# Masked k by small DMAs, scores in any two PSUM banks, and a new order: a four-layer attention and FFN kernel

## The chip, the cores and the metric

The kernel runs on one core of a Trainium2 chip. The metric is the device time of one execution in microseconds (us), as a median of several runs. Five engines have instruction queues of their own: TensorE (PE; its weight loads are shown as PEld), VectorE (DVE), ScalarE (ACT), GpSimd (POOL) and SyncE (SP), which here only issues DMAs.

## The reference

Four layers work on `x` of 2048 rows and 512 columns in bfloat16: attention with a memory, a gated FFN, and both again. Each adds to `x`, and each begins with a layer norm. Cut to what matters:

```python
def _A_ref(x, wq, wk, wv, wo, beta):          # 32 heads of 16, N = 4 segments of L = 512 rows
    q, k, v = ...                              # x @ wq, x @ wk, x @ wv, by head and segment
    phi = lambda t: jnp.where(t > 0, t + 1.0, jnp.exp(t))
    mask = (ar[:, None] < ar[None, :]) * -1e9  # causal inside a segment
    g = sigmoid(beta)
    M, z = 0, 0
    for s in range(N):
        p = softmax(qs @ ks.T * scale + mask)
        a_dot = p @ vs
        a_mem = (phi(qs) @ M) / (phi(qs) @ z + 1e-6)
        outs.append(g * a_mem + (1.0 - g) * a_dot)
        M = M + phi(ks).T @ vs
        z = z + phi(ks).sum(0)
    return concat(outs) @ wo

def _B_ref(x, w_gate, w_up, w_down):           # inner width 1792
    return gelu(x @ w_gate) * (x @ w_up) @ w_down

x = x + _A_ref(layernorm(x), ...)
x = x + _B_ref(layernorm(x), ...)
x = x + _A_ref(layernorm(x), ...)
x = x + _B_ref(layernorm(x), ...)
```

Both attention layers share their weights, and so do both FFNs.

## The kernel before

**Tiles.** `x_sb` holds the whole `x`, and all weights stay in SBUF. The work is cut into eight parts, k = 0 to 7: two layer pairs of four segments of 512 rows each. A part has an attention (class `Att`) and an FFN (class `Ffn`). A 512x512 projection is done in four blocks b of 128 columns; a block holds eight heads of 16.

**Scores.** A head has 16 rows of its block, and four heads are multiplied at once in four row groups of TensorE. The even heads of a block stand at rows 32j to 32j+15, so they use 16 rows of `kf` directly. The odd heads use 32 rows of `kB`, a copy of `kf` in which the rows of the even heads are zero. Before, `k_done` makes that copy on GpSimd: it multiplies the 128x512 block by the column `maskB` (L539), after the block's eviction from PSUM. `score_ready` demands it for the odd heads alone. For k = 0, `q`, `kf` and `kB` lie in `wd_sb`, which is loaded later; other parts rotate over three sets.

**From scores to output.** Rounds of scores go into pairs of PSUM banks; two rounds fill two pairs. Before, a pair is banks 2p and 2p+1 (`ps_pairs`). ScalarE takes the exponential of a pair in one instruction over 1024 columns (L1199), GpSimd zeroes the part above the diagonal (`affine_select`, L1205), and a "flush" multiplies five rounds by v (L809). DVE transposes and divides the result (L824 to L839) and adds the memory's part (L842). `wo` adds to `x_sb` (L879). Rows are then normed: statistics on DVE (L405, L413), a power on GpSimd (`rs`, L418 and L423), and `xn` on DVE (L435). `xn` is transposed into `xnT` by a DMA on SP (`turn_later`), or on TensorE for three of the parts (L467).

**phi.** `e` = exp on ScalarE (L596), cut at 1 by GpSimd or DVE (L614; `phi_pool` tells below which part it is DVE), and summed with the positive part on DVE (L600). phi of k is transposed by DMA (`phik`), and so is the memory's output (`amT`).

**FFN.** Gate products are evicted to `gel_sb` by DVE or ScalarE (L366, L367; `evict` leaves it to whichever is planned to be first) and then turned into gelus over several tiles at once (`gelu_tiles`, L991). The last `direct` gates of a part take the gelu straight from PSUM (L917). Products with up are multiplied on DVE (L939).

**What sets the order.** All engines run in an order that `order` writes out before the program is built. It keeps a clock for each engine (`Engine`, `Clocks`), posts each step with a planned duration and a slack, and lets each engine take what comes next by planned time. TensorE goes on as long as an item is ready and a bank free. If nothing is, it emits a dummy matmul on `warm` (a "fill"). Products run in the array's tiling at that moment: whole (L379) or as four column groups of 32 (L376); scores use row groups (L793), flushes column groups. The numbers of `POLICY` are slacks and due times of the planner. On the chip the order is fixed, and semaphores do the waiting; SP's DMAs too are issued strictly in the planned order, and nearly all of them on one queue.

Of the kernel before, what the change touches and what calls it, by code (L numbers as in the profile page):

```python
# [54 lines left out]
    flush_wait=-1.813, piece_slack=1.086, kb_slack=2.08, mem_slack=-2.073, margin=1.389, qk_due=0.513,  # L55
    e_q=-0.257, e_k=1.032, exp_slack=0.902, e_slack=10.959, phi_slack=4.283, gelu_slack=1.187, act_evict=3.627,
    first_evict=4.817, gate_step=0.01, up_due=0.388, up_step=0.027, down_due=2.499, down_step=0.058,
    upd_due=-0.151, v0_due=-1.527, x1_at=10.541, x2_at=16.065, x3_at=40.015, cut_slack=6.049, direct=1,
    gelu_tiles=3, kb_dve=0, phi_pool=1, rounds=2, early=1, starve=0.518, cap=4, fuse=1)


class Engine:
# [4 lines left out]
    def __init__(self, overlap=0.0):  # L67
        self.free, self.overlap, self.jobs, self.table = 0.0, overlap, [], "exp"
        self.only = None
# [17 lines left out]
    def serve(self, now):  # L87

        self.jobs = [j for j in self.jobs if not j[4]]
        jobs = [j for j in self.jobs if not self.only or j[3] in (None, self.only)]  # L90
        if not jobs:
            return False
        start = max(self.free, min(j[0] for j in jobs) + self.LATENCY)
        if start > now:
            return False
        job = min((j for j in jobs if j[0] + self.LATENCY <= start + 0.03), key=lambda j: j[0] + j[1])
        ready, _, steps, table, taken = job
        taken.append(1)
        self.jobs.remove(job)
        t = ready  # L100
        if table and table != self.table:
            self.free += 1.28
            self.table = table
        for cost, emit, told in steps:
            t = max(self.free, t + self.LATENCY) + cost
            self.free = t - self.overlap
            if emit:
                emit()
            if told:
                told(t)  # L110
        return True


class Clocks:
# [6 lines left out]
    def __init__(self):  # L121
        self.pe = 0.0
        self.mode = "whole"
        self.act, self.dve, self.pool, self.sp = Engine(0.09), Engine(0.07), Engine(), Engine()
        self.engines = (self.dve, self.act, self.pool, self.sp)
        self.later, self.seq, self.waiting = [], 0, []
        self.dma, self.fills, self.stalls = 0.0, [], []
        self.ev = {}
# [103 lines left out]
def order(pol, nc, cst, seg, wrk, psp, A_x, A_wq, A_wk, A_wv, A_wo, A_beta, B_x, B_w_gate, B_w_up, B_w_down, out):  # L232
# [34 lines left out]
    pieces = [(14.0, 512, lambda: load_x(2)), (27.0, 512, lambda: load_x(3))]  # L267
# [17 lines left out]
    nc.vector.memset(warm[:], 1.0)  # L285

    ps_all = psp.tile([P, BANKS, L], F32, tag="ps", bufs=1, name="ps")
    ps_pairs = ps_all[:].rearrange("p (a b) c -> p a (b c)", b=2)
# [20 lines left out]
    maskB = cst.tile([P, 1], F32, name="maskB")  # L309
    nc.vector.reduce_sum(out=maskB[:], in_=bd[:, 16:P:32], axis=mybir.AxisListType.X)  # L310
# [81 lines left out]
    class Norm:  # L392
# [46 lines left out]
        def row(self, j, i, ready):  # L439
            xn = Box(lambda: self.normed(j, i))  # L440

            def landed(t):
                xn_slots.back(i, t)
                self.left -= 1
                if not self.left:
                    ev[self.key] = t

            def told(t):
                if self.key in BY_PE:
                    items.append(self.turn_item(j, xn, t, landed))  # L450
                else:
                    turn_later(t, self.slack, lambda: self.xnT[:, :, j * P:(j + 1) * P], lambda: xn()[:], landed,
                           pol.margin)

            ck.dve.post(ready, self.slack, (0.46, xn, told))
# [34 lines left out]
    class Att:  # L490
# [12 lines left out]
        def add_items(self):  # L503
# [5 lines left out]
            def first():  # L509
                if k:  # L510
                    self.q, self.kf, self.kB = (seg.tile([P, KT, L], BF16, tag=f"{n}{k % SETS}", bufs=1, name=n)
                                                for n in ("q", "kf", "kB"))
                else:
                    self.q, self.kf, self.kB = (wd_sb[:, KT * i:KT * (i + 1), :] for i in range(3))
                return True
# [19 lines left out]
            def k_done(b, ps, at=None):  # L535
                def told(t):
                    ev["k", k, b] = t
                    eng, job, cost = (nc.vector, ck.dve, 0.345) if k < pol.kb_dve else (nc.gpsimd, ck.pool, 1.566)
                    job.post(t, pol.kb_slack if k else NORMAL, (cost, lambda: eng.tensor_scalar(  # L539
                        out=self.kB[:, b, :], in0=self.kf[:, b, :], scalar1=maskB[:, 0:1], scalar2=None,  # L540
                        op0=ALU.mult), lambda t2: ev.update({("kB", k, b): t2})))
                    if s < NSEG - 1:
                        before = ("mem", k - 1) if s else ("mem", k - 2) if k else ("xnTa", k + 1)
                        e_jobs.append((k + pol.e_k + 0.03 * b, t, lambda: before in ev,
                                       lambda r, sl: self.phi(b, "k", r, sl)))

                if at is not None:
                    told(at)
                else:
                    evict(ps, lambda: self.kf[:, b, :], lambda: ps()[:], told)  # L550
# [4 lines left out]
            def v(j):  # L555
# [4 lines left out]
                def done():  # L560
# [6 lines left out]
                            lambda: ck.has(("xnTa", k)) and (k <= SETS or ("flush", k - SETS, 3, 1) in ev),  # L567
# [17 lines left out]
        def phi(self, b, which, ready, slack):  # L585
            def take(i):
# [29 lines left out]
                def summed(t):  # L616
                    ck.dve.post(t, pol.phi_slack, (0.75 if which == "q" else 0.83, add, told))

                def made(t):
                    if self.k < pol.phi_pool:  # L620
                        ck.dve.post(t, pol.phi_slack, (0.32, cut(nc.vector), None),
                                    (0.75 if which == "q" else 0.83, add, told))
                    else:
                        ck.pool.post(t, pol.cut_slack, (1.566, cut(nc.gpsimd), summed))
# [154 lines left out]
        def score_round(self, t, places):  # L779
# [5 lines left out]
            for ki, q0, n, c0 in PIECES[i]:  # L785
                for j in range(4):
# [6 lines left out]
                    nc.tensor.matmul(ps_all[:, 2 * pair + unit // 2, o:o + n], lhsT=lhsT[rows, b, P * ki:P * ki + P],  # L793
# [3 lines left out]
        def flush_item(self, b, par, places, masked):  # L797
# [16 lines left out]
            def done():  # L814
# [35 lines left out]
                def put():  # L850
                    steps = [(0.706, back, None if self.s else there)]
                    if self.s:
                        steps.append((0.447, add, there))
# [3 lines left out]
                if par:  # L857
                    steps += [(0.355, inverse, None), (0.7, scale, kept)]
# [185 lines left out]
    first_scale(2, 4)  # L1044
    n0.first_xn = [n0.normed(0, 0), n0.normed(1, 1)]
# [24 lines left out]
    ck.pe, ck.act.free, ck.dve.free, ck.pool.free, ck.sp.free = 8.8, 9.45, 8.9, 6.2, 7.2  # L1070
# [4 lines left out]
    later_constants()  # L1075
    for at, kb, piece in pieces:
# [12 lines left out]
    norm_of_input(1, pol.x1_at, 0.5)  # L1089
    norm_of_input(2, pol.x2_at, 1.0)  # L1090
    norm_of_input(3, pol.x3_at, 1.0)
# [4 lines left out]
    score_pairs = set()  # L1096
# [14 lines left out]
    def free(bank, t):  # L1111
        return banks[bank] <= t

    def free_pairs():
        return [p for p in range(BANKS // 2) if free(2 * p, ck.pe - 0.05) and free(2 * p + 1, ck.pe - 0.05)]
# [4 lines left out]
    def rounds_now():  # L1120

        if not streams:
            return 0
        ready = 0
        for k, t in streams[:pol.rounds]:
            if not att[k].score_ready(t):
                break
            ready += 1
        n = min(len(free_pairs()), len(slot_free), ready)
        if n >= 3 and len(streams) != 4:  # L1130
            return 3
        if n >= 2 and len(streams) != 3 and (streams[0][0] < pol.early or len(streams) in (2, 4) or backlog() < pol.starve):
# [3 lines left out]
    def pick():  # L1136

        got = [i for i in range(BANKS) if free(i, ck.pe)]
        mine = len({i // 2 for i in range(BANKS) if banks[i] > ck.pe and i // 2 not in score_pairs})
        half = [i for i in got if not free(i ^ 1, ck.pe)]  # L1140
        if half:
            return min(half, key=lambda i: (-banks[i ^ 1], banks[i]))
        if got and (mine < pol.cap or not streams):
            return max(got, key=lambda i: i)
        return None
# [8 lines left out]
    def score(n):  # L1154
        pairs = free_pairs()[:n]
# [26 lines left out]
        groups = [[p] for p in range(n)] if n == 2 or not pol.fuse else [[2], [0, 1]] if pol.fuse == 1 else [[0, 1], [2]]  # L1182
        for group in groups:
            jobs, parts = [], []
            for p in group:
                pair, slot = pairs[p], slots[p][1]
                score_pairs.add(pair)
                slot_users[slot] = len(users[p])
                banks[2 * pair] = banks[2 * pair + 1] = 1e9
# [8 lines left out]
            def exp(p0=p0, p1=p1, s0=s0, s1=s1):  # L1198
                nc.scalar.activation(  # L1199
                    out=pt_all[:, s0:s1 + 1:max(s1 - s0, 1), :, :].rearrange("p s u c -> p s (u c)"),  # L1200
                    in_=ps_pairs[:, p0:p1 + 1:max(p1 - p0, 1), :], func=ACT.Exp, scale=SCALE)
# [6 lines left out]
            def told(a, parts=parts, jobs=jobs):  # L1208
                for pair, _ in parts:
                    score_pairs.discard(pair)  # L1210
                    banks[2 * pair] = banks[2 * pair + 1] = a
# [19 lines left out]
    while streams or items or opened or ck.busy():  # L1231
# [16 lines left out]
        if bank is not None:  # L1248
# [6 lines left out]

            if streams:
# [65 lines left out]
```

## Time and profile before

| | |
|---|---|
| Median of 3 runs | 563.16 us (561.08 to 563.27) |
| The profiled execution | 561.81 us, span 560.1 us |
| TensorE busy | 542.6 us (97%), 9193 matmuls |
| DVE busy | 449.8 us (80%) |
| ScalarE busy | 450.9 us (81%) |
| GpSimd busy | 323.8 us (58%) |
| Exponentials of scores (ACT L1199) | 320, mean 1026 ns |
| Masks on the diagonal (POOL L1205) | 320, mean 589 ns |
| Cuts of e on GpSimd (POOL L614) | 44, mean 1520 ns |
| DMA share | 20.1% of 16 engines on the main queue |
| Granted TensorE clock | 1.0 |

The profile is one execution. "Busy" counts an engine's instructions; a wait is idle time. The chain that ended last is followed back from the last instruction, so a share in it says how much of the span hung on that engine. Some matmul records are missing from the trace: 9193 of 9234 are there.

### The profile page before, as it was taken

What the parts mean: (1) busy time and instruction counts of PE and PEld (TensorE: products, weight loads), DVE (VectorE), ACT (ScalarE), POOL (GpSimd) and SP (SyncE); (2) the same over time, 40 slices, a digit from 0 to 9 for tenths busy, and PEclk for the clock granted to TensorE, in tenths of its full rate; (3) what the DMA queues carried; (4) which work ended last, traced back from release to release, by engine and by line L of the source; (5) the groups of instructions that cost most, each with busy time, mean ns of one, the idle gap of its engine ahead of it and who ended that gap; (6) DMA issues with size and microseconds to landing.
All of it is one profiled execution on the core that took longest, in us unless ns stands there. A gap on an engine that the chain in (4) does not pass through costs nothing.

```text
span 560.1 us, 21158 instructions
## 1 busy us (share of the span) xinstructions
PE 542.6 (97%) x9193; PEld 271.0 (48%) x9234; DVE 449.8 (80%) x821; ACT 450.9 (81%) x533; POOL 323.8 (58%) x438
## 2 busy tenths in 40 slices
PE   7999999999999999999999999999999999999997
PEld 3444454444445444444444444445445445555544
DVE  4999899979998699789698887988976877886332
ACT  5899999999798978999999699998899986730230
POOL 3699899278724997258881389835785344200000
PEclk9999999999999999999999999999999999999999
DMA  7155801600231023400321030210310004100001
GB/s 225 32 117 169 180 2 31 180 2 2 40 68 12 3 30 61 64 2 12 49 40 22 20 59 4 48 23 12 57 43 22 2 3 78 40 3 21 19 1 37
DMA packets 64925, 25.76 MB, mean 46 GB/s; under 512 B 54336, under 2 KB 64832, under 8 KB 64832
## 3 DMA queue, kind: packets, MB, share of 16 engines
q1 hardware_dynamic: 64400, 24.13, 20.1%
q8 instruction: 72, 1.18, 0.9%
q10 hardware_dynamic: 432, 0.27, 0.2%
q14 instruction: 21, 0.17, 0.1%
HBM read 9.71 MB, written 2.10 MB: 21 GB/s over the span
## 4 chain that ended last, share of the span: by engine, by line
PE 69%; DVE 20%; DMA 4%; issue 3%; ACT 2%; POOL 1%; SPq 0%; ACTq 0%; DVEq 0%
PE ps L376 37%; PE ps L379 19%; PE ps L793 6%; PE ps L809 4%; DVE st L405 3%; DVE xn L435 3%; DVE x_sb L879 2%; DVE byq L824 2%; DMA phik<-e 2%; ACT pt L1199 2%; DVE gel_sb L366 1%; DVE ab L832 1%; DMA wv_sb<-in_A_wv_dram 1%; DVE phiq L600 1%; PE ps L665 1%
## 5 line engine op out<-in xcount | busy, mean ns | idle before, releaser
L1199 ACT ACTIVATE pt<-ps 128x1024 bf16<-128x1024 f32 x320 | 309.7, 1026 | 36.3 <-PE ps L793 32.4
L1205 POOL TENSOR_SCALAR_AFFINE_SELECT pt<-pt 128x512 bf16<-128x512 bf16 (+1 forms) x320 | 184.1, 589 | 132.5 <-ACT pt L1199 131.7
L939 DVE TENSOR_TENSOR gel_sb<-gel_sb,ps 128x512 bf16<-128x512 bf16 x112 | 74.5, 683 | 28.4 <-PE ps L379 17.1
L376 PE MATMUL ps<-wd_sb,gel_sb 128*32 128x512 bf16 (+1 forms) x1296 | 75.2, 370 | 0.0
L614 POOL TENSOR_SCALAR e<-e 128x512 bf16<-128x512 bf16 x44 | 66.9, 1520 | 5.8 <-ACT e L596 4.5
L879 DVE TENSOR_TENSOR x_sb<-x_sb,ps 128x512 bf16<-128x512 bf16 (+1 forms) x68 | 43.2, 645 | 30.9 <-PE ps L376 17.0
L376 PE MATMUL ps<-xnT,wg_sb 128*32 128x512 bf16 x1056 | 64.4, 380 | 0.6 <-DVE gel_sb L366 0.4
L376 PE MATMUL ps<-xnT,wu_sb 128*32 128x512 bf16 x1128 | 64.8, 379 | 0.0
L824 DVE STREAM_TRANSPOSE byq<-ps 128x512 f32<-128x512 f32 x64 | 45.1, 706 | 13.4 <-PE ps L809 12.9
L539 POOL TENSOR_SCALAR kB<-kf,maskB 128x512 bf16<-128x512 bf16 x28 | 46.5, 1661 | 8.5 <-DVE kf L366 8.0
L366 DVE CAST gel_sb<-ps 128x512 bf16<-128x512 f32 x57 | 38.1, 680 | 12.8 <-PE ps L376 5.9
L376 PEld LDWEIGHTS <-gel_sb 128*32 128x32 bf16 x1296 | 32.8, 96 | 29.2 <-issue 5.6
L376 PEld LDWEIGHTS <-wu_sb 128*32 128x32 bf16 x1128 | 30.3, 97 | 28.6 <-issue 2.4
L991 ACT ACTIVATE gel_sb<-gel_sb 128x1536 bf16<-128x1536 bf16 (+1 forms) x35 | 43.4, 1304 | 0.1
L379 PE MATMUL ps<-xnT,wg_sb 128*128 128x512 bf16 x170 | 41.9, 379 | 1.1 <-issue 0.5
L809 PE MATMUL ps<-pt,vaug 128*32 128x256 bf16 (+1 forms) x1344 | 40.8, 256 | 0.0
L405 DVE BATCH_NORM_STATS2 st<-x_sb 128x6 f32<-128x512 bf16 x60 | 40.5, 675 | 0.4
L376 PEld LDWEIGHTS <-wg_sb 128*32 128x32 bf16 x1056 | 27.1, 96 | 26.1 <-issue 5.7
L379 PE MATMUL ps<-xnT,wu_sb 128*128 128x512 bf16 x157 | 37.1, 379 | 0.8 <-issue 0.5
L435 DVE TENSOR_SCALAR xn<-x_sb,mv,rs 128x512 bf16<-128x512 bf16 x64 | 34.2, 592 | 2.7 <-POOL rs L423 2.2
L809 PEld LDWEIGHTS <-vaug 128*32 128x32 bf16 x1344 | 30.5, 97 | 11.4 <-issue 3.9
L793 PE MATMUL ps<-q,kf 16*128 16x256 bf16 (+1 forms) x672 | 31.1, 255 | 1.9 <-ACT pt L1199 1.3
(129 smaller groups left out, 757.2 us busy)
## 6 DMA issues: line engine op xcount, KB each, us to landing
wg_sb<-in_B_w_gate_dram SPq DMA_DIRECT2D x8, 224.0 KB, 5.1
wu_sb<-in_B_w_up_dram SPq DMA_DIRECT2D x8, 224.0 KB, 4.4
wd_sb<-in_B_w_down_dram SPq DMA_DIRECT2D x7, 256.0 KB, 3.1
x_sb<-in_A_x_dram SPq DMA_DIRECT2D x3, 512.0 KB, 6.8
out_dram<-x_sb SPq DMA_DIRECT2D x12, 128.0 KB, 1.7
xnT<-xn SPq DMA_TRANSPOSE x48, 2.5
wv_sb<-in_A_wv_dram SPq DMA_DIRECT2D x1, 512.0 KB, 6.9
wo_sb<-in_A_wo_dram SPq DMA_DIRECT2D x4, 128.0 KB, 3.0
```

Source lines behind the costliest of these rows:

```text
L376: nc.tensor.matmul(out[r], lhsT=lhsT[:, r], rhs=rhs, start=start, stop=stop, tile_position=(0, 32 * c))
L379: nc.tensor.matmul(out, lhsT=lhsT, rhs=rhs, start=start, stop=stop)
L405: nc.vector.bn_stats(out=self.st6[:, 0, :], in_=x_sb[:, self.tt0 + j, :])
L435: nc.vector.tensor_scalar(out=xn[:], in0=x_sb[:, self.tt0 + j, :], scalar1=self.mv[:, j, 0:1], scalar2=self.rs[:, j, :], op0=ALU.subtract, ...
L614: return lambda: eng.tensor_scalar(out=e[0][:], in0=e[0][:], scalar1=1.0, scalar2=None, op0=ALU.min)
L793: nc.tensor.matmul(ps_all[:, 2 * pair + unit // 2, o:o + n], lhsT=lhsT[rows, b, P * ki:P * ki + P], rhs=self.q[rows, b, q0:q0 + n], start= ...
L809: nc.tensor.matmul(ps()[32 * j:32 * j + 32, q0:q0 + n], lhsT=self.vaug[:, ki, h * (DH + 1):h * (DH + 1) + 32], rhs=pt_all[:, slot, unit, c ...
L824: nc.vector.transpose(out=self.byq[:, par, :, :].rearrange("p a c -> p (a c)"), in_=ps()[:])
L879: ck.dve.post(ck.made(), slack, (0.15 + 0.00104 * (c1 - c0), lambda: nc.vector.tensor_tensor(out=xt, in0=xt, in1=ps()[:, 0:c1 - c0], op=AL ...
L939: ck.dve.post(ck.made(), NORMAL, (0.683, lambda: nc.vector.tensor_tensor(out=g, in0=g, in1=ps()[:], op=ALU.mult), lambda t: (ps.read(t), e ...
L1199: nc.scalar.activation(out=pt_all[:, s0:s1 + 1:max(s1 - s0, 1), :, :].rearrange("p s u c -> p s (u c)"), in_=ps_pairs[:, p0:p1 + 1:max(p1 ...
L1205: nc.gpsimd.affine_select(out=half, in_=half, pattern=[[0, w], [1, P]], compare_op=ALU.is_ge, fill=0.0, base=0, channel_multiplier=-1)
```

## The change

It has three parts and a new plan.

1. `k_done` no longer multiplies on GpSimd. The three rotating `kB` tiles are made once (`kBs`) and zeroed by GpSimd at the start (`memset` of 128x2048 each); the part of `wd_sb` that serves for k = 0 is zeroed by DVE. Then four DMAs for each block, posted on SP, copy 16 rows of `kf` each, the odd heads' alone. `maskB` and its reduction are gone.
2. Any two free PSUM banks can form a pair of scores. The exponential reads two banks a step apart; `pick` gives the bank that has been free longest, and rounds come two at a time.
3. The planner knows durations that depend on the other engine: `Slowed(alone, more)` adds `more` where DVE and GpSimd are planned to use their port at the same time. Loads of `x` are planned by other landing times, v of part 0 waits for a planned 12.4 us, and the `POLICY` numbers are new, among them `direct` 1 to 3, `gelu_tiles` 3 to 4 and `phi_pool` 1 to 0.

All engines get a new order by this. The products are the same. Counted in the two instruction orders:

| Instructions | before | after |
|---|---|---|
| Dummy matmuls on `warm`, column groups of 32 | 80 | 68 |
| Dummy matmuls on `warm`, whole array, 512 and 256 columns | 21, 24 | 21, 24 |
| Changes of the array's tiling on TensorE | 352 | 341 |
| DVE evictions of gate, q, k, v blocks | 107 | 115 |
| ACT evictions of the same | 78 | 56 |
| Gelus straight from PSUM (ACT) | 21 | 35 |
| Gelus over `gel_sb` (ACT): 512, 1536, 2048 columns | 7, 28, 0 | 0, 7, 14 |
| Cuts of e on DVE, on GpSimd | 4, 44 | 0, 48 |
| Multiplications by `maskB` on GpSimd | 32 | 0 |
| Copies of 16x512 into `kB` (SP) | 0 | 128 |
| Other DMAs on SP | 153 | 153 |

The diff, cut to its core:

```diff
-    gelu_tiles=3, kb_dve=0, phi_pool=1, rounds=2, early=1, starve=0.518, cap=4, fuse=1)
+    direct=3, gelu_tiles=4, phi_pool=0, rounds=2, early=7.036, starve=0.398, ahead=0.994, near=-4.825, cap=3)
...
+class Slowed(float):
+    def __new__(cls, alone, more):
+        self = super().__new__(cls, alone)
+        self.more = more
+        return self
...
-            t = max(self.free, t + self.LATENCY) + cost
+            t = max(self.free, t + self.LATENCY)
+            if isinstance(cost, Slowed):
+                if self.rival.port > t + 0.1:
+                    t += cost.more
+                self.port = t + cost
+            t += cost
...
+    nc.vector.memset(wd_sb[:, 2 * KT:3 * KT, :], 0.0)
...
-    maskB = cst.tile([P, 1], F32, name="maskB")
-    nc.vector.reduce_sum(out=maskB[:], in_=bd[:, 16:P:32], axis=mybir.AxisListType.X)
+    kBs = [cst.tile([P, KT, L], BF16, name=f"kB{i}") for i in range(SETS)]
...
-            ck.dve.post(ready, self.slack, (0.46, xn, told))
+            ck.dve.post(ready, self.slack, (Slowed(0.405, 0.17), xn, told))
...
             def k_done(b, ps, at=None):
+                def kb_sent(t):
+                    t2 = max(t + 1.9, ck.dma + 1.2)
+                    ev["kB", k, b] = t2
+
                 def told(t):
                     ev["k", k, b] = t
-                    eng, job, cost = (nc.vector, ck.dve, 0.345) if k < pol.kb_dve else (nc.gpsimd, ck.pool, 1.566)
-                    job.post(t, pol.kb_slack if k else NORMAL, (cost, lambda: eng.tensor_scalar(
-                        out=self.kB[:, b, :], in0=self.kf[:, b, :], scalar1=maskB[:, 0:1], scalar2=None,
-                        op0=ALU.mult), lambda t2: ev.update({("kB", k, b): t2})))
+                    for j in range(4):
+                        r = slice(32 * j + DH, 32 * j + 2 * DH)
+                        ck.sp.post(t, pol.kb_slack if k else URGENT, (0.47, lambda r=r: nc.sync.dma_start(
+                            out=self.kB[r, b, :], in_=self.kf[r, b, :]), kb_sent if j == 3 else None))
...
-                            lambda: ck.has(("xnTa", k)) and (k <= SETS or ("flush", k - SETS, 3, 1) in ev),
+                            lambda: ck.has(("xnTa", k)) and (k or ck.pe > 12.4) and (k <= SETS or ("flush", k - SETS, 3, 1) in ev),
...
-                    nc.tensor.matmul(ps_all[:, 2 * pair + unit // 2, o:o + n], lhsT=lhsT[rows, b, P * ki:P * ki + P],
+                    nc.tensor.matmul(ps_all[:, pair[unit // 2], o:o + n], lhsT=lhsT[rows, b, P * ki:P * ki + P],
...
+    for kB in kBs[1:] + kBs[:1]:
+        nc.gpsimd.memset(kB[:], 0.0)
...
+        got = sorted(free_banks(), key=lambda i: banks[i])[:2 * n]
+        got.sort()
+        pairs = [got[2 * p:2 * p + 2] for p in range(n)]
...
-                    out=pt_all[:, s0:s1 + 1:max(s1 - s0, 1), :, :].rearrange("p s u c -> p s (u c)"),
-                    in_=ps_pairs[:, p0:p1 + 1:max(p1 - p0, 1), :], func=ACT.Exp, scale=SCALE)
+                    out=pt_all[:, s0, :, :].rearrange("p (h u) c -> p h (u c)", h=2),
+                    in_=ps_all[:, p0[0]:p0[1] + 1:p0[1] - p0[0], :], func=ACT.Exp, scale=SCALE)
```

## The prediction

> **What bounds the kernel now.** I read the engine shares first, then the chain that ended last, then the stages, and at the end the single waits.
>
> ```profile
> span 560.1 us, 21158 instructions
> ...
> PE 542.6 (97%) x9193; PEld 271.0 (48%) x9234; DVE 449.8 (80%) x821; ACT 450.9 (81%) x533; POOL 323.8 (58%) x438
> ...
> PE 69%; DVE 20%; DMA 4%; issue 3%; ACT 2%; POOL 1%; SPq 0%; ACTq 0%; DVEq 0%
> ```
>
> TensorE (PE) is busy for 97% of the span and carries 69% of the chain. GpSimd (POOL), from which the change takes most work, carries 1%. So a microsecond counts only if it comes off TensorE's own work or off its idle time. The stages show where that idle time is (columns: window, its length, then busy time of PE, PEld, DVE, ACT and POOL, the granted clock, DMA share and GB/s):
>
> ```profile
> 0.00:20.00 20.00, 16.04 (x144) 7.40 (x145) 11.89 (x36) 12.36 (x21) 7.88 (x19) 1.00 0.51 159
> 20.00:100.00 80.00, 78.17 (x1483) 38.34 (x1482) 75.76 (x146) 75.21 (x95) 75.84 (x95) 1.00 0.41 95
> 100.00:480.00 380.00, 371.85 (x6732) 183.88 (x6759) 320.50 (x572) 341.65 (x391) 236.83 (x321) 1.00 0.19 36
> 480.00:540.00 60.00, 59.62 (x767) 32.58 (x768) 35.99 (x61) 20.38 (x27) 3.22 (x6) 1.00 0.03 11
> 540.00:560.10 20.10, 16.91 (x91) 8.77 (x90) 5.65 (x9) 1.30 (x3) 0.00 (x0) 1.00 0.08 27
> ```
>
> TensorE idles 4.0 us in the first 20, 3.2 in the last 20 (the last additions and stores), and 1.8 + 8.2 + 0.4 = 10.4 us in the 520 between. From 20 to 100 us all four engines are at 94% or more, GpSimd at 95%. From 100 us on GpSimd has a third of its time free. The longest waits name the pieces:
>
> ```profile
> PE ps L379 <- DMA wv_sb<-in_A_wv_dram: 2.0, 1, 2.0
> ...
> PE ps L793 <- ACT pt L1199: 1.3, 2, 0.7
> ...
> PE ps L642 <- DVE phiq L600: 1.1, 1, 1.1
> ...
> PE ps L719 <- DMA phik<-e: 0.5, 1, 0.5
> ```
>
> Half of the first stage's idle time is one wait for `wv`. No later wait is over 1.1 us, so no single repair in the middle is worth much, and there is also little that a better order could win.
>
> **TensorE's own work.** The two instruction orders hold the same products. Only the dummy matmuls on `warm` in the main loop differ: 80 quarter-array ones become 68, the rest stay. Four fill the array once, and in the trace 212 quarter-array matmuls take 11.55 us, 0.218 for four: 3 x 0.218 = 0.65 us less. The array's tiling (whole, four column groups, row groups) changes 352 times before and 341 times after. A 512-column matmul that a score round follows gives 312 ns from start to start, against 216 within one tiling, so a change costs 0.10: 11 x 0.10 = 1.1 us less. Together -1.75 us.
>
> **The start.** Before, the first scores (10.09) are followed by v, whose weights land at 12.45. After, q and k of blocks 1 and 2 come in between: 16 whole matmuls at 0.216, 3.5 us, with a score round among them, so v starts at about 14.5. Their weights, the last loads of `wq` and `wk`, land at 9.47. The 2.0 us wait is gone. ScalarE waits there as well (2.01 us, for the score round that stands behind v at 14.53); that round now comes at about 12.1, while its second exponential runs until 12.5, so ScalarE doesn't hold it up. -2.0 us.
>
> **Masked k.** Out go 32 GpSimd multiplications:
>
> ```profile
> L539 POOL TENSOR_SCALAR kB<-kf,maskB 128x512 bf16<-128x512 bf16 x28 | 46.5, 1661 | 8.5 <-DVE kf L366 8.0 <-ACT kf L367 0.4
> ...
> L539 POOL TENSOR_SCALAR wd_sb<-wd_sb,maskB 128x512 bf16<-128x512 bf16 x4 | 6.8, 1704 | 3.6 <-ACT wd_sb L1067 3.6
> ```
>
> (Count, busy time, mean ns, idle time before.) That is 53.3 us. In come four cuts of e that VectorE (DVE) had (`phi_pool` 1 to 0), 4 x 1.52 = 6.1 us, and three memsets of 128x2048. No such memset is in the trace: a 128x128 one takes 205 ns and a 128x1 one 102, which gives 0.1 + 2048 x 0.8 ns = 1.7 us; at the rate of the 128x512 multiplication it would be 6. I take 1.7, the same operation: from 7.2 us, after `rs`, to 12.4, when the first masks are due. At 6 they end at 25, and the first flush, at about 22, would slip by up to 6 us. The memset on DVE (128x1024, about 0.9 us by 128x60 at 108 ns and 128x128 at 165) lies before the first `x_sb` lands at 3.5 us. Off the chain, all of this is worth nothing by itself.
>
> **The copies.** Each multiplication becomes four 16 KB copies on SP's queue, 128 in all. SP's plain DMAs take 0.43 us to issue (median), so 55 us are added to the 161 that its 153 DMAs take now. No copy from SBUF to SBUF without transposition is in the trace. The nearest rows (size of one, then median us from issue to landing):
>
> ```profile
> wu_sb<-in_B_w_up_dram SPq DMA_DIRECT2D x8, 224.0 KB, 4.4
> ...
> xnT<-xn SPq DMA_TRANSPOSE x48, 2.5
> ...
> out_dram<-x_sb SPq DMA_DIRECT2D x8, 64.0 KB, 1.6
> ```
>
> I take 1.9 us, nearer the stores; bounds 1.5 and 5 (among weight loads). From the eviction of k to the fourth landing that makes 4 x 0.43 + 1.9 = 3.6 us, at most 6.7. Against it stands the lead: I laid the matmuls of the new order end to end at 216 ns for 512 columns and 0.1 us for each tiling change, and took the time from the last product of a k block to the first score that reads its masked copy. It is 12.3 us or more for 31 of the 32 blocks, and those cost nothing. For the first block it is 5.7: k is evicted at 10.69 (L1067), the x load ahead in the queue lands at 13.74, the copies land by 14.3 to 15, and the score comes at 15.75. Covered by 0.8 us; with the 5 us bound it would be 2.3 late.
>
> **ScalarE (ACT) and VectorE.** ScalarE loses 22 evictions (x 0.61 = 13.5 us), gains 14 gelus straight from PSUM (x 0.585 = 8.2), and its gelus over SBUF become fewer and wider: 28 x 1.475 + 7 x 0.617 = 44.1 become 14 x 1.90 + 7 x 1.475 = 36.9, with 1.90 from the step of 0.43 a tile. That is -12.5 us. VectorE gains 8 evictions (+5.4) and loses the four cuts (-1.3). It also loses some contention: `xn` takes 405 ns when GpSimd is idle and up to 823 when it isn't, and with the sums L600, L832 and L842 the excess over the undisturbed durations is 23.8 us; GpSimd gets 47 of its 324 us lighter, so I take 15%, -3.5. Net +0.6. Between scores TensorE's work outweighs ScalarE's in both orders from exponential 40 on, so the 12.5 us fall into idle time. Exponentials over two separate banks instead of neighbours move the same 1024 columns; I put them at the measured 1026 ns. At 30 ns more, 320 would make 9.6 us, inside the 12.5.
>
> **Waits in the middle.** Of the 10.4 us, 2.4 belong to one knot: at 207.3 the denominators wait 1.1 for phiq, held by GpSimd cuts of 1.5 and 1.92 us back to back, and the next score rounds wait 0.68 and 0.63 for ScalarE. With lighter GpSimd and an order that reckons with the contention I take -2.0, between -6 (most waits go) and +11 (below).
>
> **The sum.** -1.75 - 2.0 - 2.0 = -5.75 us. The profiled execution took 561.81 us (span 560.1 and 1.7 around it), the median of the runs is 563.16: 563.16 - 5.75 = 557.4.
>
> **Rivals.**
>
> *Order and queue take the place of the waits (slower).* In the new order transposes stand right behind a group of masked-k copies in some 17 places on SP. SP waits in order: a transposed `xn` or `phik` that is ready then loses 4 x 0.43 = 1.7 us, more if k's eviction is late. For it: DMA phik already ends one wait of TensorE, and a transpose sometimes takes 4 us to land and not 2.45. Against it: the leads from `wo` to gate in the new order (9.9 to 26 us) are like the old ones (8.8 to 31). Tightest is part 2 among those that transpose by DMA, 14.7, where 0.65 + 0.85 + 1.4 + 0.6 + 4 x 1.3 + 2.45 = 11.2 is needed. Six uncovered places cost 10.2 us, and with the gain of 5.75 it ends at 567.6. It decides from the fourth place on (5.75 / 1.7).
>
> *The wait comes back at another place (no change).* The first masked k arrives late, or the exponentials fall behind, and the middle keeps its 10.4: 563.16 - 1.75 = 561.4. At one copy after the other, by the stores' 1.6 us, the fourth lands at 10.7 + 6.4 = 17.1, 1.35 after it is wanted. The Trainium skill, page "DMA: Bandwidth & Descriptors", section "Rules for kernel authors", speaks against the four copies: it says that many small transfers are to be made one large one, since below 64 KB one pays mostly overhead; its section on the anatomy of a DMA puts the fixed part at about 2 us (for another issuing path). If those added up, an estimate from that page is 8 us for four and a first score 2.9 us late, 560.3 with all else as forecast. The trace speaks against adding up: two 64 KB stores issued at 519.28 and 520.81 land 1.5 us after their issue each, and weight loads issued 0.43 apart land 0.6 apart.
>
> *A larger gain.* From 20 to 100 us GpSimd, at 95%, loses 16 multiplications of 1.7, and the order packs that stretch anew. If waits there and later go too, -6 and not -2: 553.4, and down to 550 with a shorter start.
>
> **How the numbers follow.** The measurement of this kernel can tell about 0.5%, 2.8 us. My forecast, 557.4, has 0.42 (own range 554 to 560.3), the larger gain 0.16, no change 0.19, and slower 0.23, because the order was made anew everywhere and a plan that errs pays on TensorE at once. Faster: 0.42 + 0.16 = 0.58. The range goes from 550 to 569: the large gain's low end and six lost places, which leaves out about 0.15.
>
> **What would show it.** Right: no wait of TensorE for `wv`; 17 filling quarter-array groups; TensorE's span short by about 5 us, with its busy time down by about 2; GpSimd at about 282 us; copies landing within 2 us; nobody waiting long for kB. Wrong: scores waiting on kB or on DMA kf at 15 us, transposes late behind the copies, or memsets of 6 us.

## Result: 678.4 us, and the profile after

The changed kernel takes 678.37 us (median of 4 runs, 676.52 to 679.76). The kernel before, on the same chip, takes 563.21 (561.08 to 565.49). The ratio is 1.2042, 95% interval [1.1985, 1.2098]: a fifth slower, far outside the predicted range. The page of the changed kernel:

```profile
span 675.9 us, 21581 instructions
...
PE 570.2 (84%) x9384; PEld 277.3 (41%) x9384; DVE 457.4 (68%) x825; ACT 449.9 (67%) x511; POOL 279.1 (41%) x413
...
PE 66%; ACT 17%; DVE 9%; issue 4%; POOL 2%; DMA 1%; ACTq 0%; DVEq 0%; POOLq 0%
...
L1229 ACT ACTIVATE pt<-ps 128x1024 bf16<-128x1024 f32 x320 | 317.0, 1023 | 142.0 <-PE ps L814 77.8
```

No engine has notably more to do: GpSimd falls from 323.8 to 279.1, ScalarE is the same, and an exponential still takes 1023 ns. TensorE's busy time grows by 27.6 us, though its products are the same and its counted fills fewer; its mean granted clock is 0.98, where it was 1.0. The larger part of the loss is idle time. TensorE had 17.5 us of it and now has 105.7; ScalarE idles 142.0 us ahead of exponentials and carries 17% of the chain where it carried 2%. The stages (columns as before):

```profile
0.00:20.00 20.00, 13.26 (x75) 6.08 (x76) 12.46 (x24) 7.41 (x15) 9.47 (x17) 0.83 0.51 160
20.00:100.00 80.00, 63.54 (x1175) 30.59 (x1175) 58.76 (x119) 61.59 (x73) 45.33 (x67) 1.00 0.44 96
100.00:480.00 380.00, 318.70 (x5444) 149.39 (x5443) 268.82 (x479) 281.98 (x315) 177.86 (x252) 0.98 0.17 32
```

The loss is spread over the whole main loop: in the 380 us from 100 on, TensorE idles 61 us where it idled 8. And the first 20 us are bad in a way of their own: 13.26 busy at a granted clock of 0.83, against 16.04 at 1.00. The list of waits (total us, times, longest):

```profile
ACT pt L1229 <- PE ps L814: 77.8, 87, 4.6
...
PE ps L392 <- ACT pt L1229: 60.6, 55, 1.8
...
DVE byq L845 <- ACT pt L1229: 26.8, 16, 4.0
...
PE ps L395 <- ACT pt L1229: 14.9, 14, 2.4
...
DVE x_sb L900 <- ACT pt L1229: 9.0, 6, 2.5
```

Projections (L392, L395), the transposes of results (L845) and the additions of `wo` (L900) wait for exponentials, and exponentials for scores. Before, TensorE's largest entry for an exponential was 1.3 us in all, and for scores (L793). That a projection waits for an exponential is natural only if it wants a bank that the exponential reads.

**Theory F (false waits).** The new exponential reads two banks a step apart, `ps_all[:, p0:p1+1:p1-p0]`. The builder that puts in the semaphores orders such an access as if it covered the banks in between as well. Counted in the built programs, for waits where one side is an exponential of scores:

| Waits | before | after: shares a bank | after: only a bank between |
|---|---|---|---|
| TensorE on an exponential | 274 | 146 | 106 |
| DVE on an exponential | 59 | 32 | 87 |
| Exponential on TensorE | 311 | 207 | 80 |
| Exponential on DVE | 60 | 60 | 69 |

Before, all 320 exponentials lie over neighbours and no wait is of the last kind. After, 128 lie 2 to 5 banks apart, and 342 waits protect a bank that the exponential doesn't touch. One example: a product of `wq` into bank 1 waits for the exponential of banks 0 and 3. The planner knows nothing of these waits.

**Theory M (memset).** VectorE at the start, before and after (start, duration, what):

```profile
7.20 0.73 DVE L435 TENSOR_SCALAR xn<-x_sb,mv,rs 128x512 bf16<-128x512 bf16 x2 [0.21 <-POOL rs L1023]
```

```profile
7.22 5.49 DVE L451 TENSOR_SCALAR xn<-x_sb,mv,rs 128x512 bf16<-128x512 bf16 x2 [0.21 <-POOL rs L1044]
```

and GpSimd after:

```profile
7.14 5.43 POOL L1067 MEMSET kB<- 128x2048 bf16 x3
```

Two `xn` take 5.49 us instead of 0.73, just as long as GpSimd's three memsets beside them. The first starts 0.08 us after the first memset and lasts 3.61 us, until the second memset has ended; the other ends with the third. The first exponential ends at 18.4 instead of 11.6. The Trainium skill, page "SBUF — State Buffer", section "Who interferes with whom", states the mechanism: VectorE in a two-port mode, which `tensor_scalar` can enter, and GpSimd share one pair of ports; whoever issues first keeps it and the other is blocked, not slowed. The trace agrees as to the block, and shows it lasting for one `xn` through two memsets in a row, not one of 1.80 us; in which mode `xn` ran, no run here shows.

**Rivals.** S: SP's queue, with the copies ahead of the transposes. P: the new plan itself is poor. The expectations call the two together Q.

### The profile page after: what moved, and what is told of

Read it like the earlier page. It is cut to its first block, busy times and chain, and to the rows that moved or that the text cites. A ratio compares the mean times of both kernels' runs of the same rounds, so it can differ in the third digit from the quotient of the medians.

```text
span 675.9 us, 21581 instructions
## 1 busy us (share of the span) xinstructions
PE 570.2 (84%) x9384; PEld 277.3 (41%) x9384; DVE 457.4 (68%) x825; ACT 449.9 (67%) x511; POOL 279.1 (41%) x413
## 4 chain that ended last, share of the span: by engine, by line
PE 66%; ACT 17%; DVE 9%; issue 4%; POOL 2%; DMA 1%; ACTq 0%; DVEq 0%; POOLq 0%
PE ps L392 34%; PE ps L395 17%; ACT pt L1229 17%; PE ps L814 7%; PE ps L830 4%; DVE byq L845 1%; DVE gel_sb L382 1%; DVE x_sb L900 1%; PE ps L686 1%; POOL pt L1235 1%; DVE xn L451 1%; PE ps L740 1%; DVE gel_sb L960 1%; DVE am L696 1%; DVE phiq L621 0%
## 5 line engine op out<-in xcount | busy, mean ns | idle before, releaser
L1229 ACT ACTIVATE pt<-ps 128x1024 bf16<-128x1024 f32 x320 | 317.0, 1023 | 142.0 <-PE ps L814 77.8
L392 PE MATMUL ps<-xnT,wu_sb 128*32 128x512 bf16 x1328 | 79.2, 380 | 11.9 <-ACT pt L1229 11.9
L392 PE MATMUL ps<-xnT,wg_sb 128*32 128x512 bf16 x1116 | 71.0, 386 | 17.2 <-ACT pt L1229 17.2
L900 DVE TENSOR_TENSOR x_sb<-x_sb,ps 128x512 bf16<-128x512 bf16 (+1 forms) x68 | 43.9, 650 | 56.2 <-PE ps L392 31.1
L392 PE MATMUL ps<-wd_sb,gel_sb 128*32 128x512 bf16 (+1 forms) x1168 | 65.8, 360 | 13.6 <-ACT pt L1229 13.6
L635 POOL TENSOR_SCALAR e<-e 128x512 bf16<-128x512 bf16 x48 | 72.9, 1520 | 7.0 <-ACT e L617 4.9
L845 DVE STREAM_TRANSPOSE byq<-ps 128x512 f32<-128x512 f32 x64 | 45.3, 709 | 34.0 <-ACT pt L1229 26.8
L392 PEld LDWEIGHTS <-wu_sb 128*32 128x32 bf16 x1328 | 35.9, 97 | 47.8 <-issue 17.1
L395 PE MATMUL ps<-wd_sb,gel_sb 128*128 128x512 bf16 (+1 forms) x212 | 44.4, 358 | 4.2 <-ACT pt L1229 3.9
L392 PEld LDWEIGHTS <-wg_sb 128*32 128x32 bf16 x1116 | 28.2, 97 | 47.8 <-issue 28.0
L392 PEld LDWEIGHTS <-gel_sb 128*32 128x32 bf16 x1168 | 29.5, 96 | 40.5 <-issue 22.9
L395 PE MATMUL ps<-xnT,wg_sb 128*128 128x512 bf16 x169 | 39.8, 379 | 3.5 <-ACT pt L1229 3.5
L392 PE MATMUL ps<-wo_sb,aT 128*32 128x512 bf16 x496 | 31.3, 380 | 6.7 <-ACT pt L1229 6.3
L1012 ACT ACTIVATE gel_sb<-gel_sb 128x2048 bf16<-128x2048 bf16 (+1 forms) x21 | 36.1, 1768 | 0.0
L814 PE MATMUL ps<-q,kB 32*128 32x256 bf16 (+1 forms) x672 | 32.7, 255 | 3.1 <-ACT pt L1229 2.6
```

The costliest lines, as they stand in the source:

```text
L392: nc.tensor.matmul(out[r], lhsT=lhsT[:, r], rhs=rhs, start=start, stop=stop, tile_position=(0, 32 * c))
L395: nc.tensor.matmul(out, lhsT=lhsT, rhs=rhs, start=start, stop=stop)
L635: return lambda: eng.tensor_scalar(out=e[0][:], in0=e[0][:], scalar1=1.0, scalar2=None, op0=ALU.min)
L814: nc.tensor.matmul(ps_all[:, pair[unit // 2], o:o + n], lhsT=lhsT[rows, b, P * ki:P * ki + P], rhs=self.q[rows, b, q0:q0 + n], start=True, ...
L845: nc.vector.transpose(out=self.byq[:, par, :, :].rearrange("p a c -> p (a c)"), in_=ps()[:])
L900: ck.dve.post(ck.made(), slack, (0.15 + 0.00104 * (c1 - c0), lambda: nc.vector.tensor_tensor(out=xt, in0=xt, in1=ps()[:, 0:c1 - c0], op=AL ...
```

## Experiments

Times differ a little from chip to chip, so each is given with its ratio to the kernel before in the same runs.

**1 to 3: neighbouring pairs, moved memsets, both.** Pairs 2p and 2p+1 again, with `pick` handing out single banks so as to keep pairs whole (planned anew by the changed kernel's planner):

```diff
-        n, left = len(free_banks()) // 2, len(streams)
+        n, left = len(free_pairs()), len(streams)
...
-        got = sorted(free_banks(), key=lambda i: banks[i])[:2 * n]
-        got.sort()
-        pairs = [got[2 * p:2 * p + 2] for p in range(n)]
+        pairs = free_pairs()[:n]
```

> The changed kernel, but a pair of scores is again banks 2p and 2p+1, and banks are given out as before; copies, memsets and the policy numbers stay, and the order is planned anew. It has 47 fills after the warm-up, the changed kernel 23. Theory F (false waits: an exponential over two banks that are not neighbours is ordered as if it also read the banks between them, so products and evictions there wait for it and it for them): of the 115 us lost, all but the 7 us at the start are these waits, so 678 - 108 + 24 x 0.216 = 575 us, and TensorE's waits for L1229 fall from over 100 us to about 3. Theory Q (the new order, its slacks and the 128 copies on SP lose the time): stays above 650 us, since all of that stays.

Measured: 585.13 us, 1.0407 [1.0381, 1.0432]. TensorE idles 25.1 us. That is far from Q's 650, and still 10 us above F's 575.

The three memsets spread, and no longer beside `xn` (one of the two on VectorE stands behind the gate's constants):

```diff
+    nc.vector.memset(kBs[1][:], 0.0)
+    nc.gpsimd.memset(kBs[2][:], 0.0)
...
-    for kB in kBs[1:] + kBs[:1]:
-        nc.gpsimd.memset(kB[:], 0.0)
...
+    nc.vector.memset(kBs[0][:], 0.0)
```

> The changed kernel, but of the three kB memsets only one stays on GpSimd, ahead of rs; one goes to DVE before the first statistics and one to DVE after the gate's constants. Theory M (GpSimd's memsets hold the port that DVE's xn needs: two xn take 5.49 us in place of 0.73): the first exponential ends at about 12 us and not 18.4, and the time falls by 5 to 7 us, to 672. If the start is late for another reason (loads, the copies): within 2 us of 678.

Measured: 671.65, 1.1958 [1.1921, 1.1995]. The two `xn` are back at their old duration, and the first exponential ends at 11.9:

```profile
7.29 0.73 DVE L453 TENSOR_SCALAR xn<-x_sb,mv,rs 128x512 bf16<-128x512 bf16 x2 [0.21 <-POOL rs L1046]
```

Both edits:

> Both edits, neighbouring pairs and the moved memsets. If F and M are separate and add up: 575 - 6 = 569 us. If the loss at the start is hidden by later waits once the false ones are gone, the same as with neighbouring pairs alone, 575.

Measured: 577.57, 1.0279 [1.0254, 1.0304]. So M is real and small (0.0084 and 0.0128 of 562, that is 5 to 7 us), and something in how banks are paired costs far more. But experiments 1 and 3 also have another order: 47 fills after the warm-up where the changed kernel has 23 and the kernel before 26, and TensorE's work (columns, and 0.1 us for each tiling change, both counted in the order) at 528.5 us where before has 524.7 and after 523.0. They don't separate F from P.

**4: the same order and banks, split exponentials.** This does. Only the 128 exponentials over banks that lie apart become two over one bank each; nothing else moves.

```diff
-                nc.scalar.activation(
-                    out=pt_all[:, s0, :, :].rearrange("p (h u) c -> p h (u c)", h=2),
-                    in_=ps_all[:, p0[0]:p0[1] + 1:p0[1] - p0[0], :], func=ACT.Exp, scale=SCALE)
+                dst = pt_all[:, s0, :, :].rearrange("p (h u) c -> p h (u c)", h=2)
+                if p0[1] - p0[0] == 1:
+                    nc.scalar.activation(out=dst, in_=ps_all[:, p0[0]:p0[1] + 1, :], func=ACT.Exp, scale=SCALE)
+                    return
+                for h in range(2):
+                    nc.scalar.activation(out=dst[:, h, :], in_=ps_all[:, p0[h], :], func=ACT.Exp, scale=SCALE)
```

> The changed kernel with its own order and its own banks, but the 128 exponentials over banks that are not neighbours are each done as two of 512 columns, so that no access spans a bank it doesn't read. Theory F: the 108 us go; 128 extra instructions cost ScalarE about 0.18 us each, 23 us, of which what lies on the path stays: 575 to 593 us. Theory Q, or a slow exponential over banks apart: 678 or more, with 23 us more work on ScalarE.

Measured: 564.92, 1.0049 [1.0029, 1.0068], less than the 575 to 593 of F, and no wait of the "only between" kind is left. ScalarE does more work for it:

```profile
PE 546.5 (97%) x9384; PEld 271.4 (48%) x9384; DVE 458.2 (81%) x825; ACT 446.6 (79%) x639; POOL 285.4 (51%) x413
...
L1231 ACT ACTIVATE pt<-ps 128x1024 bf16<-128x1024 f32 x192 | 192.6, 1034 | 33.4 <-PE ps L814 30.3
...
L1234 ACT ACTIVATE pt<-ps 128x512 bf16<-128x512 f32 x256 | 138.9, 615 | 8.7 <-PE ps L814 7.7
```

331.5 us of exponentials, 14.5 more than with one instruction each, and yet the kernel is 0.199 of 563, 112 us, faster. TensorE's idle time is 16.7 us, less than before the change. F holds, and P falls as the main cause: order, banks, copies and memsets are those of the changed kernel. (Of the 112.7 us between the two profiled spans, 89.0 show as TensorE's idle time. The other 23.7 show as busy time, 570.2 against 546.5, with a mean granted clock of 0.98 in the changed kernel and 0.99 here; matmul ends are modelled, and the runs don't divide this part further.)

**5: split exponentials and moved memsets.**

> The changed kernel in its own order, with the exponentials over banks apart split in two and the kB memsets moved off GpSimd's start. Theory F+M: the 7 us that moving the memsets gave twice come off 564.9 as well: 558 us, and the forecast's terms are there to be read: no wait for wv (-2), TensorE's work 1.7 us shorter; 0.5 to 1% faster than the kernel before. If without the false waits the late start is hidden in ScalarE's queue: 563 to 565.

Measured: 558.65, 0.9953 [0.9938, 0.9969], as F and M added have it. F and M together explain the whole loss. TensorE idles 15.3 us. One wait stands out, and it is the one that rival S describes:

```profile
PE ps L816 <- ACT pt L1232: 4.6, 1, 4.6
```

ScalarE and SP at that place:

```profile
68.62 0.63 ACT L619 ACTIVATE e<-q 128x512 bf16<-128x512 bf16 x1 [5.29 <-DMA phik<-e]
```

```profile
62.94 2.12 SPq L360 DMA_TRANSPOSE xnT<-xn  x1
65.12 0.56 SPq L266 DMA_DIRECT2D wu_sb<-in_B_w_up_dram  x1
65.78 1.20 SPq L360 DMA_TRANSPOSE phik<-e  x1
```

The exponential of `e` waits 5.3 us until `phik`'s transpose has read the buffer that it wants; the transpose stands in SP's queue; exponentials of scores stand behind `e`, and TensorE behind them.

**6: the second part of the change alone.** Masked k on GpSimd as before, no copies, no memsets, any two banks. First with split exponentials, then, in the same order, with one instruction each:

```diff
-                    for j in range(4):
-                        r = slice(32 * j + DH, 32 * j + 2 * DH)
-                        ck.sp.post(t, pol.kb_slack if k else URGENT, (0.47, lambda r=r: nc.sync.dma_start(
-                            out=self.kB[r, b, :], in_=self.kf[r, b, :]), kb_sent if j == 3 else None))
+                    ck.pool.post(t, pol.kb_slack if k else NORMAL, (1.566, lambda: nc.gpsimd.tensor_scalar(
+                        out=self.kB[:, b, :], in0=self.kf[:, b, :], scalar1=maskB[:, 0:1], scalar2=None,
+                        op0=ALU.mult), lambda t2: ev.update({("kB", k, b): t2})))
```

> The changed kernel with split exponentials, but part 1 undone: GpSimd multiplies by maskB again, no copies, no memsets; planned anew with 18 more fills (3.9 us) and 7 more tiling changes (0.7 us) than the changed kernel. If the copies carry a gain of their own (lighter GpSimd, less contention on DVE): over 558 + 4.6 = 563, up to 568. If the copies cost (SP in order): under 560.

Measured: 564.7, 1.0057 [1.004, 1.0074]. That lies in the first range. Against experiment 5 it is 0.0104 of 562, 5.8 us, more, and the 18 more fills and 7 more tiling changes account for 4.6 of them. What the copies save and what they cost on SP's queue, where experiment 5 loses 4.6 us, can't be told apart by this.

> Only the second and third parts of the change: kB is written by GpSimd as before, no copies and no memsets, but any two banks form a pair, 118 of 320 exponentials are over banks that lie apart, in one instruction each. The same order with those 118 split took 564.7. Theory of false waits (an access that strides over two banks is ordered as if it covered the banks between): TensorE's idle time rises from 17 to some 100 us although no copy is there, 650 to 670 us, ratio 1.16 to 1.19; waits of DVE and TensorE on exponentials lead the list. Rival (the copies on SP's queue or the memsets are what makes the separate banks dear): 565, ratio 1.00 to 1.01.

Measured: 651.87, 1.1582 [1.155, 1.1614]. Its longest waits of TensorE and of VectorE for ScalarE, with not one copy in the kernel:

```profile
PE ps L392 <- ACT pt L1225: 48.4, 44, 2.5
...
DVE byq L843 <- ACT pt L1225: 12.4, 10, 2.2
PE ps L395 <- ACT pt L1225: 12.4, 13, 1.7
```

Separate banks alone cost 0.1525 of 562, 86 us, for 118 exponentials that lie apart and 297 false waits. The changed kernel has 128, 342 and 112 us. That is about 0.3 us for a false wait in both.

**7: the copies alone.** The kernel before, with its own planner numbers, with masked k by copies and spread memsets; 0.6 us planned for each issue. Cut to the copies:

```diff
...
+                    for j in range(4):
+                        r = slice(32 * j + DH, 32 * j + 2 * DH)
+                        ck.sp.post(t, 14.086 if k else URGENT, (0.6, lambda r=r: nc.sync.dma_start(
+                            out=self.kB[r, b, :], in_=self.kf[r, b, :]),
+                            (lambda t2: ev.update({("kB", k, b): max(t2 + 1.9, ck.dma + 1.2)})) if j == 3 else None))
```

> The kernel before with part 1 of the change alone: masked k by four copies into zeroed tiles (memsets placed as in the experiment before), planned with 0.6 us an issue; pairs, policy and durations as before, order planned anew: it has 26 more filling matmuls (5.6 us) and 2 more tiling changes than the kernel before. Theory 'copies are harmless': 563 + 5.8 less up to 2 for lighter GpSimd: 566 to 569 us. The forecast's rival 'queue on SP': six or more transposes late by 2.4 us each come on top: over 580.

Measured: 569.61, 1.0152 [1.0124, 1.018]. That is just above the 566 to 569 of harmless copies and well below the 580 of the rival. TensorE waits 3.8 us for `xnT`, 2.9 for `phik` and 1.6 for `wv`; none of it for `kB`. The new order holds 26 more fills than the kernel before, and TensorE's work is 530.4. What the copies bring can't be read from this, since the order made with these planner numbers is a worse one; experiments 1, 3, 6 and 8 (18 to 24 more fills than the changed kernel, 527.5 to 528.5 of work) suffer the same.

**8: neighbours where possible.** Experiment 5 with `pick` for scores preferring neighbouring free banks, and the split's cost told to the planner: 81 splits instead of 128.

> Like the first one of this call, but pairs are formed of neighbouring banks where two are free, and the planner knows that a split exponential costs more (1.11 us against 1.024): 81 split exponentials in place of 128, order planned anew with 20 more fills (4.3 us). If the split costs the path (F, with ScalarE near its limit): 47 x 0.09 to 0.18 = 4 to 8 us less split work against 4.3 us more fills: 555 to 560. If splits cost nothing on the path: 562.

Measured: 571.29, 1.0178 [1.0153, 1.0204]. Fewer splits and a slower kernel, outside both ranges: it is 12.6 us above experiment 5. The new order holds 20 more fills (4.3 us), TensorE waits 5.2 us for `phik`, and ScalarE 8.5. It doesn't tell what a split costs by itself, only that 47 fewer of them don't make up for a poorer order.

**9 and 10: the late transpose.** First, experiment 5 with four buffers for `e` in place of three:

```diff
-                    e.append(wrk.tile([P, L], BF16, tag=f"e{i}", bufs=1, name="e"))
+                    e_used[0] += 1
+                    e.append(wrk.tile([P, L], BF16, tag=f"e{e_used[0] % 4}", bufs=1, name="e"))
```

> The changed kernel with split exponentials and moved memsets, and besides four buffers for e (exp of the gate's input) in place of three; the order is the same. Theory (a transposing DMA that stands behind the copies on SP's queue held the buffer of e, and with it ScalarE, once, for 4.6 us): that one wait of TensorE on an exponential near 70 us is gone and the time is 558.65 - 4.6 = 554, ratio to before 0.986 to 0.989. Rival (the wait only moves to the next reader of phik or to the next exponential): TensorE's idle time stays at 14 to 16 us, 557 to 559, ratio 0.993 to 0.997.

Measured: 559.34, 0.9955 [0.9938, 0.9972], the ratio that the rival gives. ScalarE no longer waits there, and the wait moved to the reader of `phik`:

```profile
PE ps L744 <- DMA phik<-e: 4.5, 1, 4.5
```

So the transpose itself is late, and one more buffer doesn't help. Then experiment 5 with the 16 loads of the gate and up weights made as 8 of twice the columns, which takes 8 issues out of SP's queue just there:

```diff
-            for h in range(2):
-                c = slice(FF * h // 2, FF * (h + 1) // 2)
-                pieces.append((37.0 + 1.6 * (8 * n + 2 * kt + h), 224, lambda sb=sb, w=w, kt=kt, c=c: load(
-                    sb[:, kt, c], w_view(w)[:, kt, c])))
+            pieces.append((37.0 + 1.6 * (8 * n + 2 * kt), 224, lambda sb=sb, w=w, kt=kt: load(
+                sb[:, kt, :], w_view(w)[:, kt, :])))
+            pieces.append((37.0 + 1.6 * (8 * n + 2 * kt + 1), 224, lambda: None))
```

> The changed kernel with split exponentials and moved memsets (three buffers for e), and besides the 16 loads of the gate and up weights made as 8 of twice the columns, at the place of the first of each two; the order of all other work is the same. With the smaller loads SP issues without a gap from 35 to 76 us and the transposes of phi of k stand in that line; TensorE lost 4.6 us there in each of two runs (once over the buffer of e, once over phik itself). Theory (SP's issuing is short there: 8 issues of 0.58 fewer are 4.6 us, about half of them ahead of the late transpose): phik's transposes are issued 2 to 4 us earlier, the wait of 4.6 us near 70 to 75 us shrinks to under 2, 554.5 to 556.5 us, ratio 0.987 to 0.991. Rival (the transpose is late because of its data or of the DMA engines, not of the queue): the wait stays at 4 to 5 us, 558 to 560, ratio 0.994 to 0.997; wider loads that land later would show as a wait of TensorE on wg_sb or wu_sb.

Measured: 554.19, 0.9872 [0.985, 0.9894], faster than both kernels. SP:

```profile
60.61 1.20 SPq L359 DMA_TRANSPOSE phik<-e  x1
62.25 1.74 SPq L562 DMA_DIRECT2D kB<-kf  x2
```

The transpose that was issued at 65.78 is issued at 60.61, 5.2 us earlier. It takes longer to land, 4.73 us where it took 2.82, so it lands only 3.3 us earlier; why it takes longer, no run shows. The chain of experiment 5 and of this run at that place:

```profile
65.78 2.82 DMA phik<-e
```

```profile
60.61 4.73 DMA phik<-e
```

ScalarE's wait for it falls from 5.3 to 2.1 us, and TensorE's wait behind it from 4.6 to 1.5:

```profile
PE ps L815 <- ACT pt L1231: 1.5, 1, 1.5
```

So most of the late transpose was the queue. The stages:

```profile
0.00:20.00 20.00, 18.45 (x172) 8.25 (x174) 16.25 (x42) 14.44 (x25) 9.89 (x22) 1.00 0.55 168
20.00:100.00 80.00, 77.16 (x1407) 38.64 (x1409) 74.11 (x143) 75.23 (x111) 54.64 (x76) 1.00 0.48 108
100.00:480.00 380.00, 375.52 (x7055) 187.56 (x7086) 328.43 (x582) 340.06 (x485) 214.66 (x311) 1.00 0.20 39
```

The start idles 1.55 us (4.0 before) and 100 to 480 idles 4.5 (8.2 before). With GpSimd at 68% from 20 to 100, where it was at 95%, TensorE still idles 2.8 us there, 1.5 of them in that wait.

## Why the prediction was wrong, step by step

- **"Exponentials over two separate banks ... I put them at the measured 1026 ns."** The failed step. The duration was right (1023), and duration was all that was priced; the waits that such an access brings stand in the sum at nothing, without a reason. The runs showed 342 false waits, 112 us, in their place. No rival had it. The built program could have been counted beforehand; the prediction's one row for this edit was of an engine's busy time.
- **Memsets "off the chain, ... worth nothing by itself".** The duration was again right (1.7 forecast, 1.80 to 1.94 measured, not 6), and the place was wrong: "from 7.2 us, after `rs`" is where `xn` runs, which feeds the first projections. 5 to 7 us. The paragraph on VectorE even reckons with `xn` at 405 or 823 ns by what GpSimd does, but spreads that over the kernel and doesn't apply it to this memset.
- **Copies: issue 0.43, landing 1.9.** The row of DMA issues in the changed kernel (size, median us to landing):

```profile
kB<-kf SPq DMA_DIRECT2D x112, 16.0 KB, 1.8
```

  Landing is 1.8, then. The issue takes 0.587 in the median (0.507 to 1.832 in experiment 5), so 128 copies hold SP for 75 us and not 55. The 0.43 was the median of plain DMAs of other sizes. "Nobody waiting long for kB" holds: the longest such wait of TensorE is 0.3 us in the changed kernel. In experiment 5 the first four copies are issued from 10.97 on and have landed at 14.66, inside the forecast's 14.3 to 15. The estimate from the Trainium skill, page "DMA: Bandwidth & Descriptors", section "Anatomy of one DMA", by which four copies would take 8 us, isn't borne out: these four took 3.7.
- **The slower rival (SP's queue).** It was there, not in 17 places but as one wait of 4.6 us near 70 us, and not from the copies alone: copies, weight loads and transposes share the queue. Taking 8 issues out brought the ratio from 0.9953 to 0.9872, 4.5 us. The rival's price was 10.2 us for six places; it was not what decided.
- **TensorE's work -1.75.** The counted orders bear it out (524.7 us of work before, 523.0 after), the measured busy time neither confirms nor refutes it: 542.6 before, and 541.9, 545.5 and 540.2 in experiments 5, 9 and 10, which have one and the same order of matmuls, at mean granted clocks of 0.997, 0.994 and 1.0.
- **The start -2.0.** Right once the memsets are moved: idle 4.0 becomes 1.55, and no wait for `wv` is in the list.
- **Waits in the middle -2.0.** From 20 to 540 us, 10.4 us of idle time become 7.5 in experiment 10; in experiment 5 the late transpose uses up the gain. The reading behind the term was loose: between the two cuts that the forecast calls back to back stands a mask of 0.64 us, and the waits of 0.68 and 0.63 that it counts to the same knot come at 219.1 and 220.0, some 11 us after it.
- **Engines off the path.** GpSimd at 280 was forecast at 282. ScalarE was to lose 12.5 us and lost 1.0 in the changed kernel (450.9 to 449.9) and 4.6 with the wide loads, split exponentials included. (The sum has a slip: 28 x 1.475 + 7 x 0.617 is 45.6, not 44.1, so its own terms give -14.0. In the changed kernel the busy time of the 320 exponentials alone grew by 7.3 us, 309.7 to 317.0, with 1026 and 1023 ns for one.) VectorE was to gain 0.6 and gained 5.5 in experiment 5, 1.8 of it two moved memsets. Neither decided anything.

So the forecast was a gain of 5.75 us, a ratio of 0.990. Without the two faults the change measures 0.9953, 2.6 us, less than half of it; one late transpose costs it 4.6 us of TensorE's time, a price that the forecast left to a rival. The 0.9872 of experiment 10 needs wider weight loads, which the change doesn't have; that the forecast lies between the two is luck. For the kernel that the change builds the sum was useless. What stays open: how much of the gain in experiment 10 belongs to free pairs of banks, how much to the copies and how much to the plan, as each alone was only tried in an order of its own. (Experiment 3, with neighbouring pairs, is 18 us slower than experiment 5, but 5.5 us of that are counted work of another order, and the rest isn't divided.)

## What to carry to other kernels

Price a changed access pattern twice: by its duration, and by what the builder's dependency tracking takes it to cover; a strided view over buffers that others use in turn can tie them all together, and two plain instructions can be far cheaper than one wide one. When work is moved "off the chain", ask which engine shares a port or a queue with it at that very moment. To judge an edit in a kernel whose order is planned, change it in the finished order, as in experiments 4 and 6: orders planned anew held 18 to 26 more fills here than the kernel they were made from.

## What the runs showed of the hardware that was not expected

- GpSimd memsets held up VectorE's `tensor_scalar` through more than one instruction: beside three memsets of 1.80 to 1.94 us each, two `xn` took 5.49 us where they take 0.73, the first of them lasting through two memsets.
- An exponential over two banks a step of 2 to 5 banks apart costs no more than over neighbours: the 320 of the changed kernel, 128 of them over such banks, take 1018 to 1073 ns, 1023 in the mean, against 1026 before. Two over one bank each take 615 ns each.
- A 16 KB copy from SBUF to SBUF takes SP 0.587 us to issue, as much as a 224 KB weight load does there (0.574 to 0.579 in the median), and lands in 1.8 us. The number of DMAs, not their bytes, filled the queue: in experiment 10 eight loads of 448 KB did what sixteen of 224 KB had done, and the transpose behind them was issued 5.2 us earlier. In the kernel before, the same weight loads took 0.431 and 0.464 us to issue; no run shows why they took longer in the others.
